# Folding key-value blocks into the output projection: sixteen 32x32 array tiles in place of one full array, in a linear-attention and GLU kernel

## The chip, the cores and the metric

The kernel runs on one core of one Trainium2 chip. The metric is device time in microseconds (us) for one execution of the whole program. The kernel before was timed three times: 1654.0, 1654.07 and 1654.95 us, with a median of 1654.07 us.

## What is computed

The input x has 2048 tokens of 1024 features in bf16. It goes through four residual layers, A, B, A, B, each on a layer-normed copy of x, and the two A layers share their weights, as do the two B layers.

```
def A(x, wqkv, wo):                          # 32 heads of 32 features
    q, k, v = split_heads(x @ wqkv)
    phi = lambda t: where(t > 0, t + 1, exp(t)) + 1e-6
    kv  = einsum("bhsd,bhse->bhde", phi(k), v)     # one 32x32 block per head
    z   = einsum("bhsd->bhd", phi(k))
    num = einsum("bhqd,bhde->bhqe", phi(q), kv)
    den = einsum("bhqd,bhd->bhq", phi(q), z)[..., None] + 1e-6
    return merge_heads(num / den) @ wo
def B(x, w_gate, w_up, w_down):
    return ((x @ w_gate) * (x @ w_up)) @ w_down    # 1024 -> 3584 -> 1024
x = x + A(layernorm(x)); x = x + B(layernorm(x)); and both again
```

In an A layer the kernel does not form `num` and then multiply by `wo`. It first folds each head's 32x32 block into the 32 rows of `wo` that belong to the head, which gives a matrix M of 1024 x 1024, and then computes (phi(q) / den) @ M.

## The kernel before

**Tiles.** A column block of 128 features holds four heads; there are KD = 8 such blocks. Tokens go in NG = 4 groups of 512 for the q part and in 16 tiles of 128 elsewhere. A weight slot is a tile of 128 partitions by 8 x 512 bf16; there are 13 slots (pool `wp`, L49), and normed and transposed activations (`xnT`), `wq`, `wk`, `wv`, `wo`, M and the GLU weights all take their turns in them. PSUM has eight banks: four with the tag `mm` (L209), three with the tag `kv` (L212) and one with the tag `tr` (L306).

**Order.** The order of instructions on each engine is the order in which the code calls them; each engine runs its own list in order and waits on semaphores. A tile that takes a bank or slot waits until the last reader of the earlier tile there is done.

**A layer, first part.** `kv_chunk` (L224) projects k and v, tile by tile; `kp` (L244) accumulates, for each column block, phi(k)ᵀ v and phi(k)ᵀ 1 in the three `kv` banks. `wq` is loaded in this part in the first A layer (L282, plan step 20 of 64), `wo` at step 36 (L283). For the second A layer all six weight tiles are loaded by L446 to L450, just before the last down-projection of the B layer ahead of it.

**A layer, second part** (L359 to L385). A loop over i with 32 q steps. In step i the code issues, in this order: `den_step(i-4)`, `q_step(i)`, `fold(i-4)` in steps 4 to 11, `out_step(i-12)` from step 12 on. A `q_step` is eight matmuls into an `mm` bank and then phi: an Exp on ScalarE (L216) and two VectorE operations (L217, L218). A `den_step` is one matmul with zb into a `kv` bank (L341), a Ln on ScalarE that reads that bank (L343), an Exp (L344) and a VectorE multiplication (L347). An `out_step` is eight matmuls with M (L354).

In step 0 `finish_kv` (L294) reads the three banks on VectorE: it copies the sums z, writes `kvm` (the 128x128 products times a mask of four 32x32 blocks on the diagonal) and writes `zb` (the mask times z). In step 3 `tr_kv` (L305) transposes the eight `kvm` blocks into the `tr` bank, and ScalarE copies them to `kvT` (L309). Each `fold(c)` (L313) is two matmuls of the full 128x128 array, one per half of `wo`'s columns, into two `kv` banks (L318), and two copies to M, one on ScalarE (L320) and one on VectorE (L322). Eight calls of `fold` make sixteen matmuls per A layer, in which three of every four 32x32 blocks of the stationary operand are zeros.

**GpSimd** works only at the start of the kernel (masks, constants). SyncE (SP) issues all weight loads and the transposing DMAs of the normed activations, in one queue.

Of the kernel before, what the change touches and what calls it, by code (L numbers as in the profile page):

```python
# [11 lines left out]
F32 = mybir.dt.float32  # L12
# [3 lines left out]
def kernel(  # L16
# [11 lines left out]
    nc = tc.nc  # L28
    P = 128
# [3 lines left out]
    KD = D // P  # L33
# [4 lines left out]
    NB = 512  # L38
    FB = F // NB
    FPB = NB // P  # L40
    DC = D // NB
# [9 lines left out]
    work = ctx.enter_context(tc.tile_pool(name="work", bufs=2))  # L51
    psum = ctx.enter_context(tc.tile_pool(name="psum", bufs=4, space=bass.MemoryType.PSUM))
# [3 lines left out]
    wqkv_v = A_wqkv.rearrange("(k p) n -> p k n", p=P)  # L56
# [10 lines left out]
    def wslot(name):  # L67
        return wp.tile([P, KD, NB], BF16, tag="w", name=name)

    def load_cols(view, n, name, parts=1):  # L70
        w = wslot(name)
        kk = KD // parts
        for i in range(parts):
            nc.sync.dma_start(out=w[:, i * kk:(i + 1) * kk, :],
                              in_=view[:, i * kk:(i + 1) * kk, n * NB:(n + 1) * NB])
        return w
# [6 lines left out]

    def load_A(which):
        return [load_cols(wqkv_v, which * DC + n, "w" + "qkv"[which]) for n in range(DC)]

    def load_wo():
        return [load_cols(wo_v, n, "wo") for n in range(DC)]
# [5 lines left out]
    wA = {}  # L94
# [30 lines left out]
    VW = P + 1  # L125
# [85 lines left out]
    def kv_tile(name, w=NB):  # L211
        return psum.tile([P, w], F32, tag="kv", name=name, bufs=3)  # L212
# [7 lines left out]
    def layer_A(li, preload_B):  # L220
# [34 lines left out]
        def at(step, f, *args):  # L255
            plan.setdefault(step, []).append((f, args))

        NCH = 2 * DC * TPG
# [13 lines left out]
        if li == 0:  # L272
            m = DC * TPG
            chunks[0:2 * m] = chunks[m:2 * m] + chunks[0:m]
            chunks[1], chunks[2] = chunks[2], chunks[1]
            at(0, first_stats, 3, 0)
            at(0, first_norm, 2)
            at(0, first_stats, 3, 1)
            at(1, pe_tr_tile, 2)
            at(2, first_norm, 3)  # L280
            at(3, pe_tr_tile, 3)
            at(NCH + 4, lambda: wA.update(q=load_A(0)))  # L282
            at(2 * NCH + 4, lambda: wA.update(o=load_wo()))  # L283
        for i, (t, n) in enumerate(chunks):
            kv_chunk(t, n, second_tile if li == 0 and i == 0 else None)
# [4 lines left out]
        kvT = work.tile([P, KD, P], BF16, tag="kvT", name="kvT", bufs=1)  # L290
        zb = work.tile([P, KD, P], BF16, tag="zb", name="zb", bufs=1)
        z = work.tile([P, KD], F32, tag="z", name="z", bufs=1)

        def finish_kv():  # L294
            for b in range(3):
                nb = min(3, KD - 3 * b)
                src = kvp[b][:, 0:nb * VW].rearrange("p (c f) -> p c f", f=VW)
                nc.vector.tensor_copy(out=z[:, 3 * b:3 * b + nb], in_=src[:, :, P])
                for j in range(nb):
                    nc.vector.tensor_tensor(out=kvm[:, 3 * b + j, :], in0=src[:, j, 0:P], in1=mask[:], op=ALU.mult)  # L300
            for c in range(KD):
                nc.vector.tensor_scalar(out=zb[:, c, :], in0=mask[:], scalar1=z[:, c:c + 1], scalar2=None,
                                        op0=ALU.mult)

        def tr_kv():  # L305
# [4 lines left out]

        M = []

        def fold(c):  # L313
            if not M:
                M.extend(wslot("M") for _ in range(DC))
            for n in range(DC):
                ps = kv_tile("mps")
                nc.tensor.matmul(out=ps[:], lhsT=kvT[:, c, :], rhs=wA["o"][n][:, c, :], start=True, stop=True)  # L318
                if n == 0:
                    nc.scalar.copy(out=M[n][:, c, :], in_=ps[:])  # L320
                else:
                    nc.vector.tensor_copy(out=M[n][:, c, :], in_=ps[:])  # L322

        pq = {}
        pqs = {}
# [12 lines left out]
        def den_step(g, c):  # L338
            p = pq.pop((g, c))
            dps = kv_tile("dps")  # L340
            nc.tensor.matmul(out=dps[:], lhsT=zb[:, c, :], rhs=p[:], start=True, stop=True)  # L341
            r = work.tile([P, G], F32, tag="r", name="r", bufs=2)
            nc.scalar.activation(out=r[:], in_=dps[:], func=ACT.Ln, bias=eps6[:], scale=1.0)  # L343
            nc.scalar.activation(out=r[:], in_=r[:], func=ACT.Exp, scale=-1.0)  # L344
            if c % 4 == 0:
                pqs[(g, c // 4)] = hp.tile([P, HC, G], BF16, tag="h", name="pqs")
            nc.vector.tensor_tensor(out=pqs[(g, c // 4)][:, c % 4, :], in0=p[:], in1=r[:], op=ALU.mult)  # L347
# [9 lines left out]
                                    in1=ps[:], op=ALU.add)  # L357

        LAG, OLAG = 4, 12  # L359
        NQ = NG * KD  # L360
        for i in range(NQ + OLAG):
            if i >= LAG and i - LAG < NQ:
                den_step(*divmod(i - LAG, KD))
            if i < NQ:
                q_step(*divmod(i, KD))
            if i == 0:
                for t in range(NT - TPG, NT):
                    kp(t)
                finish_kv()
                preload_B("p")  # L370
            if i == 3:
                tr_kv()
            if 4 <= i < 4 + KD:
                fold(i - 4)
            if i >= OLAG:
                out_step(*divmod(i - OLAG, KD))
            if i in (14, 17, 25, 33):
                preload_B({14: "pr", 17: "r", 25: "r", 33: "rrr"}[i])
            for u in range(TPG):
                if i == 20 + 2 * u:  # L380
                    ln_stats(li + 1, (u,))
                if i == 21 + 2 * u:
                    ln_norm(li + 1, u)
                if i == 22 + 2 * u:
                    tr_tile(li + 1, u)  # L385
# [25 lines left out]
    def layer_B(li, stream):  # L411
        last = li == 3
        for g in range(NG):
            xnT = xnTs[(li, g)]
            hT = []
            nl, ng = (li, g + 1) if g + 1 < NG else (li + 1, 0)
            for f in range(KF):
                fb, j = divmod(f, FPB)
                if j == 0:
                    wg, wu = stream.have.pop((g, fb))  # L420
                gp = mm_tile("gp")
                for k in range(KD):
                    nc.tensor.matmul(out=gp[:], lhsT=wg[:, k, j * P:(j + 1) * P], rhs=xnT[:, k, :],  # L423
                                     start=(k == 0), stop=(k == KD - 1))
                up = mm_tile("up")
                for k in range(KD):
                    nc.tensor.matmul(out=up[:], lhsT=wu[:, k, j * P:(j + 1) * P], rhs=xnT[:, k, :],  # L427
                                     start=(k == 0), stop=(k == KD - 1))
                gs = work.tile([P, NB], F32, tag="gs", name="gs", bufs=2)
                nc.scalar.copy(out=gs[:], in_=gp[:])  # L430
                if f % HC == 0:
                    hT.append(hp.tile([P, HC, G], BF16, tag="h", name="hT"))
                nc.vector.tensor_tensor(out=hT[f // HC][:, f % HC, :], in0=gs[:], in1=up[:], op=ALU.mult)  # L433
                if j == FPB - 1:
                    stream.pair()
                    stream.rows()
                for u in range(TPG if nl < 4 else 0):
                    t = ng * TPG + u
                    if f == 6 + 4 * u:
                        ln_stats(nl, (t,))  # L440
                    if f == 7 + 4 * u:
                        ln_norm(nl, t)
                    if f == 8 + 4 * u:
                        tr_tile(nl, t)
            xnTs.pop((li, g))
            if g == NG - 1 and not last:  # L446
                wA["k"] = load_A(1)
                wA["v"] = load_A(2)
                wA["q"] = load_A(0)
                wA["o"] = load_wo()  # L450
            for tl in range(TPG):
                t = g * TPG + tl
                cuts = [(n * NB, (n + 1) * NB) for n in range(DC)]
                if last and t == NT - 1:
                    cuts[-1:] = [(D - NB, D - NB // 2), (D - NB // 2, D)]
                for lo, hi in cuts:
                    ps = kv_tile("dn", hi - lo)
                    for f in range(KF):
                        nc.tensor.matmul(out=ps[:], lhsT=hT[f // HC][:, f % HC, tl * P:(tl + 1) * P],  # L459
                                         rhs=stream.wd[f // 4][:, f % 4, lo:hi],  # L460
                                         start=(f == 0), stop=(f == KF - 1))
                    nc.vector.tensor_tensor(out=X[:, t, lo:hi], in0=X[:, t, lo:hi], in1=ps[:], op=ALU.add)  # L462
                    if last:
                        nc.sync.dma_start(out=o_view[:, t, lo:hi], in_=X[:, t, lo:hi])
# [47 lines left out]
```

## Time and profile before

| what | value |
|---|---|
| median of the three timed runs | 1654.07 us |
| the profiled execution's own time | 1654.75 us |
| its span in the trace | 1652.9 us, so 1.85 us lie around it |
| TensorE busy | 1646.7 us, 7864 matmuls |
| VectorE busy | 559.3 us |
| ScalarE busy | 368.0 us |
| GpSimd busy | 1.6 us in 17 instructions |
| `mps` matmuls of the fold (L318) | 32, duration of one 379 ns |
| second part of the first A layer | from 126.35 us on |
| its steps with folds | 135.8 to 156.7 us |
| the same steps of the second A layer | up to 976.4 us |

A matmul of 512 columns is shown with a duration of 379 ns, but matmuls are pipelined: eight of one `q_step` and the matmuls after them start one every 0.216 us. A time "from start to start" is therefore what a matmul costs, and its duration is how late its result is. The same holds, less strongly, for ScalarE and VectorE, where a new operation starts a little before the one ahead of it has ended. Timelines give the start in us from the beginning of the span, the duration, the engine, the line, the operation and the tiles; in brackets stands idle time before it, and who ended it.

### The profile page before, as it was taken

To read this page: it belongs to the slowest core of one execution; us is meant where nothing else is said; L and a number is where in the kernel's file an instruction comes from. 1 tells how busy PE (TensorE), PEld (TensorE's weight loads), DVE (VectorE), ACT (ScalarE), POOL (GpSimd) and SP (SyncE) were. 2 spreads that over 40 slices of the span, in tenths; PEclk is the share of its full clock that TensorE was granted. 3 is DMA by queue.
4 is the path that set the end of the run, shared out by engine and by line. 5 is a ranking of instruction groups with operands and counts; after the bars stand their busy time and mean duration, and the time that the engine had idled before them with its cause. 6 is when DMAs were issued, how large, how long until landed. Compare 5 with 4: busy or idle time off the path is not lost.

```text
span 1652.9 us, 18521 instructions
## 1 busy us (share of the span) xinstructions
PE 1646.7 (100%) x7864; PEld 757.7 (46%) x7864; DVE 559.3 (34%) x985; ACT 368.0 (22%) x699; POOL 1.6 (0%) x17
## 2 busy tenths in 40 slices
PE   9999999999999999999999999999999999999999
PEld 4544444444444444444444544444444444444444
DVE  6537762311321231132155388522113212211111
ACT  4336541200210120021033375311002101100110
POOL 0000000000000000000000000000000000000000
PEclk9999999999999999999999999999999999999999
DMA  7433134631461263055132321346225514622400
GB/s 229 127 77 102 38 90 134 172 127 39 139 163 41 83 172 128 31 141 167 46 100 39 87 79 45 124 134 172 76 87 147 162 33 131 173 82 90 153 29 23
DMA packets 211250, 174.21 MB, mean 105 GB/s; under 512 B 66528, under 2 KB 202080, under 8 KB 211168
## 3 DMA queue, kind: packets, MB, share of 16 engines
q1 hardware_dynamic: 210880, 172.64, 36.2%
q8 instruction: 61, 1.00, 0.2%
q10 hardware_dynamic: 288, 0.39, 0.1%
q14 instruction: 21, 0.17, 0.0%
HBM read 153.09 MB, written 4.19 MB: 95 GB/s over the span
## 4 chain that ended last, share of the span: by engine, by line
PE 99%; DMA 0%; SPq 0%; ACT 0%; issue 0%; DVE 0%
PE dn L459 23%; PE up L427 23%; PE gp L423 23%; PE ps L230 13%; PE ops L354 7%; PE ps L333 7%; PE kvp L248 1%; PE dps L341 1%; PE mps L318 0%; DMA wv<-in_A_wqkv_dram 0%; SPq L97 0%; PE pt L180 0%; PE pt L308 0%; ACT xnT L182 0%; SPq L65 0%
## 5 line engine op out<-in xcount | busy, mean ns | idle before, releaser
L423 PE MATMUL gp<-xnT,wg 128*128 128x512 bf16 x1792 | 423.3, 379 | 0.0
L427 PE MATMUL up<-xnT,wu 128*128 128x512 bf16 x1792 | 423.3, 379 | 0.0
L459 PE MATMUL dn<-wd,hT 128*128 128x512 bf16 (+1 forms) x1820 | 388.1, 376 | 0.0
L433 DVE TENSOR_TENSOR hT<-gs,up 128x512 bf16<-128x512 f32 x224 | 154.0, 688 | 567.0 <-PE up L427 567.0
L430 ACT COPY gs<-gp 128x512 f32<-128x512 f32 x224 | 131.4, 586 | 945.8 <-PE gp L423 945.8
L459 PEld LDWEIGHTS <-hT 128*128 128x128 bf16 x1820 | 178.1, 98 | 209.0
L423 PEld LDWEIGHTS <-wg 128*128 128x128 bf16 x1792 | 175.4, 98 | 211.4
L427 PEld LDWEIGHTS <-wu 128*128 128x128 bf16 x1792 | 175.3, 98 | 211.4
L462 DVE TENSOR_TENSOR X<-X,dn 128x512 bf16<-128x512 bf16 (+1 forms) x65 | 44.1, 679 | 341.9 <-PE dn L459 341.9
L230 PEld LDWEIGHTS <-xnT 128*128 128x128 bf16 x1024 | 99.7, 98 | 120.2 <-ACT xnT L182 1.1
L333 PE MATMUL ps<-xnT,wq 128*128 128x512 bf16 x512 | 120.3, 379 | 0.0
L354 PE MATMUL ops<-M,pqs 128*128 128x512 bf16 x512 | 118.3, 379 | 0.0
L230 PE MATMUL ps<-wv,xnT 128*128 128x512 bf16 x512 | 112.8, 379 | 1.4 <-DMA wv<-in_A_wqkv_dram 0.8
L230 PE MATMUL ps<-wk,xnT 128*128 128x512 bf16 x512 | 112.6, 379 | 0.0
L216 ACT ACTIVATE m<-ps 128x512 f32<-128x512 f32 x128 | 76.4, 597 | 158.3 <-PE ps L230 130.4
L217 DVE TENSOR_SCALAR m<-m 128x512 f32<-128x512 f32 x128 | 54.1, 422 | 82.6 <-ACT m L216 81.8
L354 PEld LDWEIGHTS <-pqs 128*128 128x128 bf16 x512 | 50.1, 98 | 60.4
L333 PEld LDWEIGHTS <-wq 128*128 128x128 bf16 x512 | 50.0, 98 | 60.1 <-issue 0.6
L146 DVE BATCH_NORM_STATS2 st<-X 128x6 f32<-128x512 bf16 x120 | 76.7, 681 | 0.0
L343 ACT ACTIVATE r<-dps,eps 128x512 f32<-128x512 f32 x64 | 44.3, 692 | 54.1 <-PE dps L341 54.1
L347 DVE TENSOR_TENSOR pqs<-pq,r 128x512 bf16<-128x512 bf16 x64 | 43.8, 685 | 31.4 <-ACT r L344 31.4
L241 ACT CAST vb<-ps 128x512 bf16<-128x512 f32 x64 | 37.6, 588 | 62.1 <-PE ps L230 62.1
(45 smaller groups left out, 384.3 us busy)
## 6 DMA issues: line engine op xcount, KB each, us to landing
wg<-in_B_w_gate_dram SPq DMA_DIRECT2D x56, 1024.0 KB, 5.2
wu<-in_B_w_up_dram SPq DMA_DIRECT2D x56, 1024.0 KB, 6.9
wd<-in_B_w_down_dram SPq DMA_DIRECT2D x14, 1024.0 KB, 5.6
wk<-in_A_wqkv_dram SPq DMA_DIRECT2D x4, 1024.0 KB, 7.7
wq<-in_A_wqkv_dram SPq DMA_DIRECT2D x4, 1024.0 KB, 7.3
wo<-in_A_wo_dram SPq DMA_DIRECT2D x4, 1024.0 KB, 7.6
out_dram<-X SPq DMA_DIRECT2D x31, 128.0 KB, 1.7
X<-in_A_x_dram SPq DMA_DIRECT2D x14, 256.0 KB, 8.5
```

The lines of the kernel that those rows point to most:

```text
L146: nc.vector.bn_stats(out=st[:, c, :], in_=X[:, t, c * FMAX:(c + 1) * FMAX])
L216: nc.scalar.activation(out=m[:], in_=ps[:], func=ACT.Exp)
L217: nc.vector.tensor_scalar(out=m[:], in0=m[:], scalar1=1.0, scalar2=1e-6, op0=ALU.min, op1=ALU.add)
L230: nc.tensor.matmul(out=ps[:], lhsT=xnT[:, k, tl * P:(tl + 1) * P], rhs=w[:, k, :], start=(k == 0), stop=(k == KD - 1))
L333: nc.tensor.matmul(out=ps[:], lhsT=w[:, k, j * P:(j + 1) * P], rhs=xnT[:, k, :], start=(k == 0), stop=(k == KD - 1))
L343: nc.scalar.activation(out=r[:], in_=dps[:], func=ACT.Ln, bias=eps6[:], scale=1.0)
L354: nc.tensor.matmul(out=ps[:], lhsT=pqs[(g, c // 4)][:, c % 4, tl * P:(tl + 1) * P], rhs=M[n][:, c, :], start=(c == 0), stop=(c == KD - 1))
L423: nc.tensor.matmul(out=gp[:], lhsT=wg[:, k, j * P:(j + 1) * P], rhs=xnT[:, k, :], start=(k == 0), stop=(k == KD - 1))
L427: nc.tensor.matmul(out=up[:], lhsT=wu[:, k, j * P:(j + 1) * P], rhs=xnT[:, k, :], start=(k == 0), stop=(k == KD - 1))
L430: nc.scalar.copy(out=gs[:], in_=gp[:])
L433: nc.vector.tensor_tensor(out=hT[f // HC][:, f % HC, :], in0=gs[:], in1=up[:], op=ALU.mult)
L459: nc.tensor.matmul(out=ps[:], lhsT=hT[f // HC][:, f % HC, tl * P:(tl + 1) * P], rhs=stream.wd[f // 4][:, f % 4, lo:hi], start=(f == 0), st ...
```

## The change

The fold uses the array as sixteen independent tiles of 32x32, each with its own position (32h, 32j). One call of the new `fold(r)` works on four column blocks (cc says which four) and one half n of `wo`'s columns. Tile (h, j) multiplies head h of column block 4cc + j with that head's 32 rows of `wo` and writes partitions 32j to 32j+31 of bank h. So one call fills four banks: three with the tag `kv` and the one with the tag `tr`. Two are copied to M by ScalarE and two by VectorE. There are four calls per A layer, with 64 small matmuls in place of 16 full ones.

The rows of M then stand in another order: within four column blocks, heads are ordered by h first and j second. To match, the columns of `wq` are put in the same order: `load_wq` loads each half of `wq` into a slot (`wqr`) and GpSimd copies it, in eight copies of 128x512, to a second slot (`wq`). The sums z are put in that order (`zn`) by sixteen GpSimd copies of 32x2 before `zb` is made.

The calls are moved: `fold` now stands in steps 5, 7, 9 and 11 and comes after `den_step` and before `q_step` of the step; it was after `q_step` in steps 4 to 11. In `finish_kv` the three copies of z now come ahead of all `kvm` operations.

```diff
+    def load_wq():
+        ws = []
+        for n in range(DC):
+            raw = load_cols(wqkv_v, n, "wqr")
+            w = wslot("wq")
+            for k in range(KD):
+                nc.gpsimd.tensor_copy(out=w[:, k, :].rearrange("p (h j d) -> p h j d", h=4, j=4),
+                                      in_=raw[:, k, :].rearrange("p (j h d) -> p h j d", h=4, j=4))
+            ws.append(w)
+        return ws
...
-            at(NCH + 4, lambda: wA.update(q=load_A(0)))
+            at(NCH + 4, lambda: wA.update(q=load_wq()))
...
+        zn = work.tile([P, KD], F32, tag="zn", name="zn", bufs=1)
         def finish_kv():
             for b in range(3):
                 nb = min(3, KD - 3 * b)
                 src = kvp[b][:, 0:nb * VW].rearrange("p (c f) -> p c f", f=VW)
                 nc.vector.tensor_copy(out=z[:, 3 * b:3 * b + nb], in_=src[:, :, P])
+            for h in range(4):
+                for j in range(4):
+                    nc.gpsimd.tensor_copy(out=zn[32 * j:32 * j + 32, h:KD:4], in_=z[32 * h:32 * h + 32, j:KD:4])
+            for b in range(3):
+                nb = min(3, KD - 3 * b)
+                src = kvp[b][:, 0:nb * VW].rearrange("p (c f) -> p c f", f=VW)
                 for j in range(nb):
                     nc.vector.tensor_tensor(out=kvm[:, 3 * b + j, :], in0=src[:, j, 0:P], in1=mask[:], op=ALU.mult)
             for c in range(KD):
-                nc.vector.tensor_scalar(out=zb[:, c, :], in0=mask[:], scalar1=z[:, c:c + 1], scalar2=None,
+                nc.vector.tensor_scalar(out=zb[:, c, :], in0=mask[:], scalar1=zn[:, c:c + 1], scalar2=None,
                                         op0=ALU.mult)
...
-        def fold(c):
+        def fold(r):
             if not M:
                 M.extend(wslot("M") for _ in range(DC))
-            for n in range(DC):
-                ps = kv_tile("mps")
-                nc.tensor.matmul(out=ps[:], lhsT=kvT[:, c, :], rhs=wA["o"][n][:, c, :], start=True, stop=True)
-                if n == 0:
-                    nc.scalar.copy(out=M[n][:, c, :], in_=ps[:])
+            cc, n = divmod(r, DC)
+            mps = [kv_tile("mps") for _ in range(3)]
+            mps.append(psum.tile([P, NB], F32, tag="tr", name="mps", bufs=1))
+            for j in range(4):
+                for h in range(4):
+                    q = slice(32 * h, 32 * h + 32)
+                    nc.tensor.matmul(out=mps[h][32 * j:32 * j + 32, :], lhsT=kvT[q, 4 * cc + j, q],
+                                     rhs=wA["o"][n][q, 4 * cc + j, :], start=True, stop=True,
+                                     tile_position=(32 * h, 32 * j))
+            for h in range(4):
+                if h % 2:
+                    nc.scalar.copy(out=M[n][:, 4 * cc + h, :], in_=mps[h][:])
                 else:
-                    nc.vector.tensor_copy(out=M[n][:, c, :], in_=ps[:])
+                    nc.vector.tensor_copy(out=M[n][:, 4 * cc + h, :], in_=mps[h][:])
...
+        FOLD = [5, 7, 9, 11]
         for i in range(NQ + OLAG):
             if i >= LAG and i - LAG < NQ:
                 den_step(*divmod(i - LAG, KD))
+            if i in FOLD:
+                fold(FOLD.index(i))
             if i < NQ:
                 q_step(*divmod(i, KD))
...
-            if 4 <= i < 4 + KD:
-                fold(i - 4)
...
-                wA["q"] = load_A(0)
+                wA["q"] = load_wq()
                 wA["o"] = load_wo()
```

## The prediction

> **What bounds the kernel now.** I read the page's first part, then the chain that ended last, then the timelines of TensorE and ScalarE in the steps with folds.
>
> ```profile
> PE 1646.7 (100%) x7864; PEld 757.7 (46%) x7864; DVE 559.3 (34%) x985; ACT 368.0 (22%) x699; POOL 1.6 (0%) x17
> ...
> PE 99%; DMA 0%; SPq 0%; ACT 0%; issue 0%; DVE 0%
> ```
>
> TensorE sets the end for 99% of the span, so a us taken off its list or put into it moves the end by a us; nothing later makes up for it. The shares of the other engines are averages. What counts is the second part of the A layer, here in the second one. The first fence is TensorE, the second ScalarE.
>
> ```profile
> 964.55 0.59 PE L318 MATMUL mps<-wo,kvT 128*128 128x512 bf16 x2
> 964.99 0.38 PE L341 MATMUL dps<-pq,zb 128*128 128x512 bf16 x1
> 965.20 1.89 PE L333 MATMUL ps<-xnT,wq 128*128 128x512 bf16 x8
> 966.93 0.59 PE L318 MATMUL mps<-wo,kvT 128*128 128x512 bf16 x2
> ```
>
> ```profile
> 966.45 0.63 ACT L344 ACTIVATE r<-r 128x512 f32<-128x512 f32 x1
> 967.13 0.60 ACT L216 ACTIVATE m<-ps 128x512 f32<-128x512 f32 x1
> 967.62 0.58 ACT L320 CAST M<-mps 128x512 bf16<-128x512 f32 x1
> 968.09 0.70 ACT L343 ACTIVATE r<-dps,eps 128x512 f32<-128x512 f32 x1
> 968.83 0.63 ACT L344 ACTIVATE r<-r 128x512 f32<-128x512 f32 x1
> ```
>
> One step is 2 fold matmuls, 1 den matmul and 8 of q: 11 in 966.93 - 964.55 = 2.38 us, 0.216 us each, no gap. ScalarE takes the same 2.38 us for its four operations (966.45 to 968.83). So 34% and 22% hide that in these eight steps TensorE has no slack and ScalarE hardly any.
>
> **What is removed.** Per A layer 16 full matmuls, 16 x 0.216 = 3.46 us; per new fold, which does the work of four of them, 0.86 us. If the new fold cost nothing the kernel would win 6.9 us, no more.
>
> **What is added: a wait on a bank.** There are three `kv` banks. When the new fold starts, one holds the den result of the step before, one that of this step's `den_step`, whose matmul stands directly ahead of the fold on TensorE. The fold takes all three. Its third tile (h = 2, first j) must wait until the Ln of this den result has read its bank. TensorE runs in order, so the other 13 small matmuls, the `q_step` and all behind it wait too. Before, a fold took two banks and had the eight matmuls of `q_step` between. Let s be the start of the last matmul of the `q_step` before:
> - The Exp on that result starts 0.42 us after s: s = 965.20 + 7 x 0.216 = 966.71, Exp at 967.13.
> - Ln is next on ScalarE (no M copy lies between them now). From start to start such a pair takes 0.47 to 0.49 us (967.13 to 967.62 to 968.09); I take 0.48. Ln lasts 0.70.
> - From a read's end to TensorE's start: 0.06 us (in the first A layer the VectorE copy of 139.79 lasts 0.68, the den matmul that waits for it starts at 140.53).
>
> The third tile starts at s + 0.42 + 0.48 + 0.70 + 0.06 = s + 1.66. TensorE was through with the den matmul at s + 2 x 0.216 = s + 0.43. The wait is 1.23 us, with the first two small matmuls inside it. ScalarE is not late on top: between two folds it has 2 x (0.68 + 0.48 + 0.73) + 2 x 0.5 = 4.8 us of work, and with the waits TensorE takes about 6.2. In the first fold of a layer ScalarE is late from copying `kvT`: there its Exp starts at 138.00, Ln would end at 139.18, TensorE goes on at 139.24 and was ready at 137.53 + 0.22 = 137.75: 1.49, that is 0.26 more. In return a wait of 0.20 us per layer goes: after the two fold matmuls at 139.90 the den matmul stood at 140.53, not at 140.33. The next den steps need a bank that an M copy frees 1.7 us and more earlier; I cost that at nothing.
>
> **The small matmuls.** No row shows tiles of 32x32. After the wait 14 remain, each with its weight load.
> - Low end: all run side by side, one slot, 0.22 us.
> - High end: one after another, 14 x 0.216 = 3.02, and 0.26 to empty the array (379 - 216 = 0.16 until the last result, 0.10 for the next full weight load): 3.28 us.
> - Value: the nearest row is a short pair of weight load and matmul, `kvp` with 129 columns. The chain has 32 of them in 1.89 us:
>
> ```profile
> 128.24 1.89 PE kvp L248 x32
> ```
>
> That is 0.059 us a pair; 14 x 0.059 = 0.83, with 0.26 to empty the array 1.09 us.
>
> Two rules of the Trainium skill bear on it. "TensorE: Matmul & The Clock Gate", section "Measured speedup vs the span model", gives 660 ns for sixteen such tiles of 512 columns. Put for my 1.09 it would make the sum 3.4 us smaller. Its section "The mechanism" speaks against the change: a weight load overlaps a running matmul only when the row group differs. Tiles of one h follow each other in the same row group with another j, so there would be four rounds one after another, about 4 x 0.216 = 0.86 us with nothing for the loads, close to what I take.
>
> **GpSimd.** Before it did nothing here. The nearest rows are its smallest and largest operations:
>
> ```profile
> L119 POOL MEMSET mask<- 32x32 f32 x4 | 0.5, 117 | 0.2
> masks.py:199 POOL TENSOR_SCALAR_AFFINE_SELECT ident<-ident 128x128 bf16<-128x128 bf16 x1 | 0.3, 294 | 0.1
> ```
>
> - The sixteen `zn` copies start when z is copied, near 130.4 us, and `zb` waits behind them on VectorE, with phi of steps 1 to 3 behind it. At 117 ns they end at 132.3, when VectorE has just done its eight `kvm` (0.2 us each). The first den matmul at 135.59 needs the first `zb` (0.28 us). Cover until 135.3: 4.9 us, 0.30 us a copy. At 294 ns it just holds. I take 0; at 1 us a copy 16 - 4.9 = 11 us per layer would be lost.
> - The eight copies of one `wqr` tile: by the two rows 0.1 us and some 1.5 ns for an element of a partition, 0.9 us. In the first layer 40 plan steps of 1.73 us lie ahead of the use. In the second the last `wo` load waits for the eight, since it takes that slot, and the transposing DMAs stand behind it in SP's queue. The slots come free in the last chunk of the down-projection, from about 824 us; the next transpose is issued at 842.8. Cover 18 us, 2.3 us a copy: 0.
> - SP issues the same DMAs in the same order. VectorE may lose something beside GpSimd's copies; it has idle time there.
>
> **The sum.** Per fold 1.23 + 1.09 - 0.86 = +1.46; eight folds 11.7; first folds 2 x (0.26 - 0.20) = 0.1. Together +11.8 on the profiled execution's 1654.75, 1666.6 us. The median lies 0.68 lower: **1665.9 us**. With the low end 0.22 the sum is 8 x 0.59 + 0.1 = +4.8 (1658.9), with the high end 3.28 it is 8 x 3.65 + 0.1 = +29.3 (1683.4).
>
> **Rivals.**
> - A, the forecast: the wait holds, tiles run partly side by side, 1658.9 to 1673. Chance 0.69.
> - B: the tiles do not run side by side, so the change doesn't do what it says: 1683. For it: four tiles of one h read different rows of `wo` out of the same partitions. Against it: they lie in separate parts of the array. Anything from 1673 up to there counts here. Chance 0.14.
> - C: GpSimd's small copies are slow, `zb` comes late. From 0.30 us a copy on, each 0.1 us more costs 1.6 us per layer: 0.6 us a copy gives 1665.9 + 9.6 = 1675.5. For it: no copy of GpSimd was ever seen in this trace. Against: four memsets at 117 ns. Chance 0.08.
> - D, faster: sixteen tiles run as one slot and give back 0.86 - 0.22 = 0.64 us a fold, and the bank is free when the third tile comes. This decides at a wait of 0.64 us per fold. With none left, 8 x -0.64 = -5.1: 1649. With 0.64 it is no change. Against: Exp and Ln alone need 0.48 + 0.70 after the q result. Faster 0.04, no change 0.05.
>
> The range reaches from the low end of A to the high end of B, 1659 to 1684, and holds A, B and most of C. Within 0.2% (3.3 us, about what a measurement of this kernel can tell) of 1654.07 counts as the same: 0.05. Faster 0.04, slower 0.91.
>
> **What would show it.** In the trace after, TensorE should stand idle at every second step of the fold window, ended by ScalarE's Ln (L368), eight times about 1.2 us; from the third small matmul to the next `q_step` about 1.1 us; two steps with a fold about 6.2 us, against 4.76. If `zb` waits for GpSimd past the first den matmul, C is right. If gaps between small matmuls are near 0.2 us, B. I am wrong if the idle time before the third tile is under 0.6 us, or if TensorE has new idle time outside the fold windows.

## The result and the profile after

The changed kernel is slower: median 1659.95 us (1659.66 to 1660.13) against 1653.88 us for the kernel before (six runs now), ratio 1.0036 with a 95% interval of 1.0023 to 1.0049. That is 6.1 us more, where 11.8 were forecast. The direction and the place were right, and the time lies just inside the low end of the range; the size was about half of the forecast.

The profiled execution has a span of 1658.3 us, 5.4 more than before. Its first lines on shares hardly move (TensorE sets 98% of the chain that ended last, 99% before), so the steps with folds have to be read. TensorE's timeline of the changed kernel, two steps in the first A layer (columns: start in us, duration, engine, line, operation, tiles, form, count, and in brackets idle time and who ended it):

```profile
142.69 0.38 PE L366 MATMUL dps<-pq,zb 128*128 128x512 bf16 x1
143.00 0.39 PE L340 MATMUL mps<-wo,kvT 32*32 32x512 bf16 x2
144.11 0.43 PE L340 MATMUL mps<-wo,kvT 32*32 32x512 bf16 x14 [0.73 <-ACT r L368]
144.48 1.90 PE L358 MATMUL ps<-xnT,wq 128*128 128x512 bf16 x8
146.22 0.38 PE L366 MATMUL dps<-pq,zb 128*128 128x512 bf16 x1
146.43 1.89 PE L358 MATMUL ps<-xnT,wq 128*128 128x512 bf16 x8
148.16 0.38 PE L366 MATMUL dps<-pq,zb 128*128 128x512 bf16 x1
```

Two small matmuls start, the third stands until ScalarE's Ln (L368) has read the bank, and the other 14 start together. The 0.73 in brackets is counted from the end of the two small ones. What the wait costs is counted from where TensorE could go on: 142.69 + 0.216 = 142.91 to 144.11 is 1.20 us. Then the next `q` matmul starts 0.37 us after the third tile. Two steps take 148.16 - 142.69 = 5.47 us; before they took 4.75 (964.55 to 966.93 was one of them).

ScalarE beside it shows why the bank comes when it does:

```profile
142.89 0.60 ACT L227 ACTIVATE m<-ps 128x512 f32<-128x512 f32 x1
143.38 0.68 ACT L368 ACTIVATE r<-dps,eps 128x512 f32<-128x512 f32 x1
144.09 0.63 ACT L369 ACTIVATE r<-r 128x512 f32<-128x512 f32 x1
```

The Exp on the last q result, then the Ln on the den result, which ends at 144.06; the third tile starts at 144.11.

From the first `q` matmul to the first `out_step` the first A layer now takes 159.10 - 125.78 = 33.32 us, against 156.71 - 126.35 = 30.36; the second likewise 33.32 against 30.37. That is 5.9 us for the two. In the profiled executions the first part of the kernel, while the first loads arrive, took 0.57 us less than before, hence the 5.4 between the spans; the medians differ by 6.1.

### The profile page after: what moved, and what is told of

It reads as the page before. It is cut to its first block, busy times and chain, and to the rows that moved or that the text cites. A ratio compares the mean times of both kernels' runs of the same rounds, so it can differ in the third digit from the quotient of the medians.

```text
span 1658.3 us, 18637 instructions
## 1 busy us (share of the span) xinstructions
PE 1638.3 (99%) x7804; PEld 756.2 (46%) x7960; DVE 562.6 (34%) x985; ACT 368.2 (22%) x699; POOL 26.8 (2%) x81
## 4 chain that ended last, share of the span: by engine, by line
PE 98%; ACT 1%; issue 1%; DVE 0%
PE gp L449 23%; PE up L453 23%; PE dn L485 23%; PE ps L241 13%; PE ops L379 7%; PE ps L358 6%; PE kvp L259 1%; PE dps L366 1%; ACT r L368 0%; ACT m L227 0%; PE wps L124 0%; PE mps L340 0%; PE pt L191 0%; ACT xnT L193 0%; ACT kvT L327 0%
## 5 line engine op out<-in xcount | busy, mean ns | idle before, releaser
L368 ACT ACTIVATE r<-dps,eps 128x512 f32<-128x512 f32 x64 | 43.9, 686 | 54.1 <-PE dps L366 54.1
```

## The experiments

One theory on where the 5.9 us come from, and three rivals, went into the first four runs. **W**: the wait for the bank, 8 x 1.2 us and a little, less what the cheap small matmuls give back. Against it stood **S**, the array draining for another tile size, which would only seem to end with the Ln; **P**, small weight loads that the wait hides; and **G**, GpSimd's copies. Diffs are against the changed kernel unless another is named.

### e1_mm_bank: the wait taken away

```diff
-            mps = [kv_tile("mps") for _ in range(3)]
+            mps = [kv_tile("mps"), kv_tile("mps"), mm_tile("mps")]
```

The fold takes one of the four `mm` banks, in which a `q_step` four steps back has been read long ago.

> The third tile row of the fold takes its bank from the four mm banks, not from the kv banks; all else is as in the changed kernel. Theory W (the loss is the wait for the Ln that reads the den result of the same step, and the sixteen tiles themselves are cheap): the wait, 1.2 us in six folds and 1.46 in two, goes; a fold then costs TensorE 0.09 to change over, 0.06 for sixteen starts and 0.31 until the next q matmul, 0.46 in place of 0.86 us. 1653.9 - 8 x 0.40 - 0.4 = about 1650.3 us. Theory S (the idle time is the array draining for another tile size, and only seems to end with the Ln): no change, 1659.5 to 1660.5. Theory P (the weight loads of the small tiles are hidden under the wait and come to light without it, 13 loads of 0.087): about 1656 to 1659.

Measured 1650.5 us, ratio 0.9979 (0.9970 to 0.9987). TensorE's timeline of this kernel:

```profile
141.21 0.38 PE L366 MATMUL dps<-pq,zb 128*128 128x512 bf16 x1
141.52 0.43 PE L340 MATMUL mps<-wo,kvT 32*32 32x512 bf16 x16
141.89 1.90 PE L358 MATMUL ps<-xnT,wq 128*128 128x512 bf16 x8
...
145.57 0.38 PE L366 MATMUL dps<-pq,zb 128*128 128x512 bf16 x1
```

No idle time before any tile; all sixteen start within 0.43 - 0.38 = 0.05 us. A fold costs 141.89 - 141.43 = 0.46 us, of which 0.09 lie before its first matmul. W holds, S and P fall: neither a drain nor weight loads fill the place of the wait. This version is faster than both kernels.

### e2_full_array: the wait alone

```diff
-            for j in range(4):
-                for h in range(4):
-                    q = slice(32 * h, 32 * h + 32)
-                    nc.tensor.matmul(out=mps[h][32 * j:32 * j + 32, :], lhsT=kvT[q, 4 * cc + j, q],
-                                     rhs=wA["o"][n][q, 4 * cc + j, :], start=True, stop=True,
-                                     tile_position=(32 * h, 32 * j))
+            for h in range(4):
+                nc.tensor.matmul(out=mps[h][:], lhsT=kvT[:, 4 * cc + h, :],
+                                 rhs=wA["o"][n][:, 4 * cc + h, :], start=True, stop=True)
...
-                wA["q"] = load_wq()
+                wA["q"] = load_A(0)
```

The first A layer loads `wq` with `load_A(0)` too, and `zb` is made from z; `zn` and its copies are gone.

> The changed kernel's order and banks, but four full 128x128 matmuls in a fold in place of the sixteen small ones, and so no GpSimd copies and no other order of wq. Theory W: the wait stays, 1.2 us, with the first two full matmuls inside it; the two left cost 0.43. A fold costs 1.64 against 0.86 before, the first of a layer 0.25 more: 1653.9 + 6 x 0.78 + 2 x 0.83 = about 1660.2 us, as much as the change. Theories S and G (GpSimd): 1653.9 us, since neither small tiles nor GpSimd copies are left.

Measured 1660.42 us, ratio 1.0038 (1.0024 to 1.0051): the loss of the change without a single small matmul and without GpSimd. Its timeline of TensorE:

```profile
142.75 0.38 PE L359 MATMUL dps<-pq,zb 128*128 128x512 bf16 x1
...
148.28 0.38 PE L359 MATMUL dps<-pq,zb 128*128 128x512 bf16 x1
148.49 0.59 PE L334 MATMUL mps<-wo,kvT 128*128 128x512 bf16 x2
149.71 0.59 PE L334 MATMUL mps<-wo,kvT 128*128 128x512 bf16 x2 [0.62 <-ACT r L361]
150.13 1.89 PE L351 MATMUL ps<-xnT,wq 128*128 128x512 bf16 x8
```

The third matmul starts 149.71 - 148.49 = 1.22 us after TensorE was ready, as with the tiles. Two full matmuls run inside the wait, and the two behind it take 0.42, against 0.37 for fourteen small ones. That is why the tiles of the change bring almost nothing there: beside the wait they save 0.42 - 0.37 = 0.05 us a fold, and without it 0.86 - 0.46 = 0.40.

### e3_gpsimd_only: GpSimd's copies in the kernel before

```diff
+                nc.gpsimd.tensor_copy(out=w[:, k, :].rearrange("p (j h d) -> p h j d", h=4, j=4),
+                                      in_=raw[:, k, :].rearrange("p (j h d) -> p h j d", h=4, j=4))
...
+                    nc.gpsimd.tensor_copy(out=zn[32 * j:32 * j + 32, h:KD:4], in_=z[32 * j:32 * j + 32, h:KD:4])
```

Against the kernel before: `load_wq`, `zn` and the new order of `finish_kv` are added, but each copy keeps the old order, so the fold is as it was. The small copies here stay in their partitions.

> The kernel before with GpSimd's copies alone: wq goes through a second slot in eight copies per half and z through sixteen small copies, all in the old order, so that the fold needs no change. Theory W: the copies are hidden, 1653.6 to 1654.4 us. Theory G (part of the 6 us is zb, which waits for GpSimd on VectorE, or the slots): 1655 to 1658 us.

Measured 1654.15 us against 1653.87, ratio 1.0000 (0.9991 to 1.0009). Of G's 1655 to 1658 us only the lowest edge lies within this interval, which ends at 1655.4. The trace of the changed kernel leaves nothing for that edge: 5.9 us more in the two second parts and 0.57 less at the start already make 5.3 of the 5.4 us between the spans. So G falls.

### e4_split_q: the fold inside its q_step

```diff
+                if between is not None and k == 4:
+                    fold(between)
...
-            if i in FOLD:
-                fold(FOLD.index(i))
             if i < NQ:
-                q_step(*divmod(i, KD))
+                q_step(*divmod(i, KD), FOLD.index(i) if i in FOLD else None)
```

> The fold of the changed kernel stands inside its q_step, after five of the eight matmuls; banks as in the changed kernel. Theory W: 5 x 0.216 = 1.08 us of q matmuls cover nearly all of the 1.2 us wait for the Ln, and three are left (0.65) before the next den matmul, which needs the bank that ScalarE's M copy frees; some 0.2 us of wait may be left there. About 1652 us. Theory S: 1659.5 to 1660.5. Theory P: 1655 to 1658.

Measured 1652.67 us, ratio 0.9992 (0.9983 to 1.0001): the loss is gone, and a gain over the kernel before is not clear of noise. The banks are those of the change; only what lies between the den matmul and the fold is different. In the timeline the fold's sixteen start without idle time, and the first den matmul behind a fold waits a little for ScalarE's M copy:

```profile
138.14 0.72 PE L340 MATMUL mps<-wo,kvT 32*32 32x512 bf16 x16
138.79 0.60 PE L358 MATMUL ps<-xnT,wq 128*128 128x512 bf16 x2
139.60 0.38 PE L368 MATMUL dps<-pq,zb 128*128 128x512 bf16 x1 [0.20 <-ACT M L345]
...
141.54 0.38 PE L368 MATMUL dps<-pq,zb 128*128 128x512 bf16 x1
...
146.07 0.38 PE L368 MATMUL dps<-pq,zb 128*128 128x512 bf16 x1
```

In this first fold of the layer, where ScalarE is late, 0.72 in place of the 0.43 of e1_mm_bank shows that 0.29 us of the wait for the Ln is left too (in the later folds, 0.47 us each, 0.04). In the two layers that is 0.6 of the 0.7 us by which W was too low, a difference that is itself within the noise of this run.

### e5_h_outer: the order of the sixteen

Against e1_mm_bank the two loops of the fold are exchanged: h is the outer one.

> As e1_mm_bank, but the sixteen tiles go in another order: four of one row group (same h) one after another, then the next row group. Theory T (all sixteen tiles are independent, what counts is only one change of the tile size in and one out): no change against e1_mm_bank, 1650.2 to 1650.8 us. Theory R (a weight load must wait for a running matmul in its row group): of the sixteen, twelve wait for the one ahead, 12 x 0.216 = 2.6 us a fold, 8 x 2.6 = 21 us more, about 1671 us.

Measured 1650.56 us, ratio 0.9980 (0.9970 to 0.9989), the same as e1_mm_bank.

```profile
141.15 0.38 PE L366 MATMUL dps<-pq,zb 128*128 128x512 bf16 x1
141.46 0.43 PE L340 MATMUL mps<-wo,kvT 32*32 32x512 bf16 x16
141.83 1.90 PE L358 MATMUL ps<-xnT,wq 128*128 128x512 bf16 x8
...
145.51 0.38 PE L366 MATMUL dps<-pq,zb 128*128 128x512 bf16 x1
```

The fold takes 141.83 - 141.46 = 0.37 us from its first matmul to the next of `q`, as there. R falls by 20 us.

### e6_twice: sixteen more without another change of tile size

```diff
-            for j in range(4):
+            for j in [0, 1, 2, 3] * 2:
```

Against e1_mm_bank; each tile's matmul is issued a second time.

> As e1_mm_bank, but each of the sixteen small matmuls is issued twice (the second writes the same result again), to see what sixteen more cost without a further change of tile size. Theory T: the second matmul of a tile must wait until the first has streamed its 512 columns, 0.216 us a fold, 8 x 0.216 = 1.7 us more, 1652.2 us; so of the 0.46 us of a fold about 0.25 is the change of tile size. Theory I (only starting them costs, 16 x 0.0035 us): 1650.9 us. Rival: weight loads of an occupied tile cannot be hidden, 16 x 0.087 = 1.4 us a fold: 1661 us.

Measured 1652.3 us, ratio 0.9990 (0.9981 to 1.0000), 1.8 us above e1_mm_bank.

```profile
141.55 0.38 PE L366 MATMUL dps<-pq,zb 128*128 128x512 bf16 x1
141.86 0.65 PE L340 MATMUL mps<-wo,kvT 32*32 32x512 bf16 x32
142.44 1.90 PE L358 MATMUL ps<-xnT,wq 128*128 128x512 bf16 x7
...
146.12 0.38 PE L366 MATMUL dps<-pq,zb 128*128 128x512 bf16 x1
```

From the fold's first matmul to the next of `q` it is 142.44 - 141.86 = 0.58 us, 0.21 more than with sixteen. So sixteen more small matmuls cost as much as one full one. If the first sixteen cost the same, the rest of a fold, 0.46 - 0.21 = 0.25 us, goes to the change of tile size in and out. How much of that is emptying the array and how much the next full weight load is not shown.

### e7_after_q: the fold behind its q_step, where it was before

```diff
-            if i in FOLD:
-                fold(FOLD.index(i))
             if i < NQ:
                 q_step(*divmod(i, KD))
+            if i in FOLD:
+                fold(FOLD.index(i))
```

> As the changed kernel with its banks, but the fold stands after q_step, as in the kernel before. Theory W: eight q matmuls cover the wait for the Ln; but all three kv banks are then full of fold results when the next den matmul follows at once, and it waits for ScalarE's M copy: the copy starts behind the Exp of the q_step, some 0.6 us after the fold's start, and lasts 0.58; the den matmul waits about 0.85 us. A fold costs 0.46 + 0.85 against 0.86: 1653.9 + 8 x 0.45 - 0.4 = about 1657 us. Rival (one wait only, that for the Ln): 1650.5 us, as e1_mm_bank.

Measured 1657.2 us, ratio 1.0020 (1.0011 to 1.0030).

```profile
142.30 0.38 PE L366 MATMUL dps<-pq,zb 128*128 128x512 bf16 x1
...
144.34 0.43 PE L340 MATMUL mps<-wo,kvT 32*32 32x512 bf16 x16
145.57 0.38 PE L366 MATMUL dps<-pq,zb 128*128 128x512 bf16 x1 [0.80 <-ACT M L345]
...
147.51 0.38 PE L366 MATMUL dps<-pq,zb 128*128 128x512 bf16 x1
```

The fold no longer waits, but now the den matmul right behind it does: all three `kv` banks hold fold results, and it takes the first that ScalarE has copied. One wait went and the next in line took its place.

### The runs side by side

The time of two steps, one with a fold, is read from den matmul to den matmul in each timeline; the difference from 4.75 is multiplied by the eight folds. First folds of a layer and a wait of 0.2 us in each layer of the kernel before account for most of what is left.

| kernel | two steps, us | times 8, us | measured change of the median, us |
|---|---|---|---|
| changed kernel | 5.47 | +5.8 | +6.1 |
| e1_mm_bank | 4.36 | -3.1 | -3.4 |
| e2_full_array | 5.53 | +6.2 | +6.6 |
| e4_split_q | 4.53 | -1.8 | -1.2 |
| e5_h_outer | 4.36 | -3.1 | -3.2 |
| e6_twice | 4.57 | -1.4 | -1.5 |
| e7_after_q | 5.21 | +3.7 | +3.4 |

## Why the prediction was half right

**The wait was right, in place and size.** Forecast 1.23 us per fold and 1.49 in the first of a layer; measured 1.20, and in the first, where the den matmul starts at 136.96 and the third tile at 138.64, 138.64 - 136.96 - 0.22 = 1.46.

```profile
136.96 0.38 PE L366 MATMUL dps<-pq,zb 128*128 128x512 bf16 x1
137.27 0.39 PE L340 MATMUL mps<-wo,kvT 32*32 32x512 bf16 x2
138.64 0.43 PE L340 MATMUL mps<-wo,kvT 32*32 32x512 bf16 x14 [0.98 <-ACT r L368]
```

The forecast's three numbers from ScalarE's rows (start of Exp after the last q matmul, Exp to Ln, duration of Ln) carried it. e1_mm_bank shows that it is more than the whole loss: taking it away saves 1659.95 - 1650.5 = 9.5 us, and what is left of the change wins 3.4. The full matmuls that go were right too: 4 x 0.216 = 0.86 us a fold.

**The step that failed is the value of the small matmuls**: "14 x 0.059 = 0.83, with 0.26 to empty the array 1.09 us". The trace after has 0.37 from the third tile to the next `q` matmul, and two steps take 5.47 us where about 6.2 were forecast. The term is 0.72 us too large, eight times 5.8 us, and that is the gap between +11.8 and what was measured. Two things went wrong in it:
- The row was no price for a start. The `kvp` pairs took 0.059 us each because each streams 129 columns: 129 / 512 x 0.216 = 0.054 us of it. A pair of weight load and matmul that falls on a free tile starts in far less: sixteen in 0.05 us, about 3 ns from one to the next. I took what a row lasts for what it costs to issue; the 512-column rows beside it (0.216 us, four times the columns, nearly four times the time) said so.
- Emptying the array was put at 0.26 on top of all starts. In e6_twice the change of size costs 0.25 us in and out together, of which 0.09 lie ahead of the fold and, in the changed kernel, inside the wait.

So the low end of the term (all sixteen side by side in one slot, 0.22 us) came nearer than the value taken; what it left out is the change back to the full array. With 0.37 in its place the sum is 8 x (1.23 + 0.37 - 0.86) + 0.1 = +6.0 us.

The two rules of the Trainium skill that stood beside the value pull apart. The section "Measured speedup vs the span model" of "TensorE: Matmul & The Clock Gate" was nearer: it has sixteen such tiles run together, in 660 ns; here the sixteen are through in 0.43 us, last result included. What the section "The mechanism" says, that a weight load overlaps a running matmul only in another row group, is not what these runs showed: with four tiles of one row group in a row (e5_h_outer) all sixteen still start within 0.05 us, and the fold takes 0.37 us as before.

**The costs put at nothing were nothing.** VectorE did wait for GpSimd in the changed kernel, and the den matmul did not notice: in the first A layer the first one starts 9.24 us after the first of `q` in both kernels (135.02 - 125.78 and 135.59 - 126.35). The groups of GpSimd (columns: count, busy us and mean ns, idle time before and what ended it) and the wait in the list of waits:

```profile
L93 POOL COPY wq<-wqr 128x512 bf16<-128x512 bf16 x32 | 19.4, 661 | 738.5 <-PE dn L485 694.1 <-DMA wqr<-in_A_wqkv_dram 44.4
L313 POOL COPY zn<-z 32x2 f32<-32x2 f32 x32 | 5.8, 181 | 189.8 <-DVE z L310 188.5
```

```profile
DVE zb L320 <- POOL zn L313: 2.5, 4, 0.6
```

The sixteen small copies take 3.6 us in a layer, 0.22 each from start to start, against the 0.30 at which rival C begins. The eight copies of one half of `wq` take 4.5 to 4.9 us, against a cover of 18. Rival C was rightly small, and e3_gpsimd_only settles it. Rival B is wrong: the tiles do run side by side. Rival D named the right point of decision, 0.64 us of wait a fold; with the measured 0.37 in place of 0.22 it lies at 0.86 - 0.37 = 0.49 us, and the wait was 1.20.

**What was not foreseen as a chance** is that this wait could be taken away with one bank: the forecast priced it and did not look for a free one. Four `mm` banks stood ready.

## What to carry to other kernels

When an instruction takes all buffers of a rotating set, look for the newest reader among them: if it is the step just issued, the wait is that reader's whole chain, here Exp and Ln, and it eats a gain that is smaller. Before a row is used as the price of issuing something, see whether its time scales with its size; then it is the price of streaming, and says nothing on small parallel work. And a wait that is moved rather than removed comes back at the next user of the same buffers (e7_after_q), so count the buffers, not the positions.

## What the hardware showed that was not expected

- Sixteen 32x32 matmuls of 512 columns, each with its own weight load and with different rows out of the same partitions for the four column groups, start about 3 ns apart (sixteen within 0.05 us in e1_mm_bank) and stream in the time of one full matmul (0.21 us by e6_twice). How the array is fed four streams from one set of partitions is not shown by these runs.
- The change between 128x128 and 32x32 and back costs about 0.25 us of TensorE, worked out from e1_mm_bank and e6_twice: 0.09 before the first small matmul, the rest before the next full one.
- GpSimd's copies of 32x2 numbers across partitions follow each other every 0.22 us (shown with 181 ns each), and those of 128x512 bf16 with a new order of blocks of 32 every 0.6 us or so (eight in 4.5 to 4.9 us, shown with 661 ns each).
